# Starting the first expert's first layer before the routing of a mixture-of-experts kernel is complete

## The chip, the core and the metric

The kernel runs on one core of one Trainium2 chip. The time is the device time of one execution in microseconds (us). The kernel before takes 449.11 us, the median of three runs (448.33 to 449.34).

## What is computed

Two stages follow each other. The first is a gated recurrent attention over 4 batches x 8 heads x 768 steps x 48 numbers; its output, regrouped, is a matrix `x` of 3072 rows (tokens) by 384. The second sends every row to one of eight experts, each a two-layer network of 384 to 1024 to 384:

```python
def _moe_ref(x, w_gate, w1, w2):
    logits = x @ w_gate
    expert_idx = np.argmax(logits, axis=1)
    probs = softmax(logits)                     # [shortened]
    gate_w = probs[np.arange(N), expert_idx]
    for e in range(E):                          # [shortened: the rows of e]
        h = np.maximum(x_sorted[lo:hi] @ w1[e], 0.0)
        y_sorted[lo:hi] = h @ w2[e]
    return gate_w[:, None] * y
```

With the seeded inputs the eight experts get 420, 387, 356, 354, 404, 409, 352 and 390 rows. Of the 420 rows of the first expert, 274 lie among the first 2048 tokens.

## The kernel before

**Attention.** The 3072 tokens are 24 chunks of 128. A loop over `s` runs the parts of several chunks side by side, in the order in which the program lists them: `attend(s)`, `scores(s + 1)`, `cums(s + 3)` and so on. Each chunk ends with its rows written to a buffer in device memory, `x_rows` (`x_d`), together with the negated router logits.

**Routing.** Rows are counted per expert in groups of chunks. For each chunk two one-hot matrices, `oh_r` and `oh_c`, say in which slot of which expert a token lands; a product of the two per chunk, summed over all 24 chunks in one PSUM tile (`route`), turns "slot of a token" into "token of a slot". From that the table `g_idx` of row numbers is made, and GpSimd gathers the rows of each block of 128 slots with one indirect DMA.

The slots of the experts follow one another: the first expert has room for 448 rows (three and a half blocks), the next ones for 384, 448 and so on, 26 blocks in all.

```python
caps = (448, 384, 448, 384, 416, 416, 416, 416)
...
s = NT - 1                                  # the last chunk
attend(s)
route = rps.tile([C, Dm], F32, name="cum")
while hots:
    one_hots(hots.pop(0))
tokens_of_slots(0, 9)                       # 9 products into route
slots_of(*rank_products(groups_of[-2], ...))
rows(s)
keep_rows(s)
choose(groups_of[-1])
one_hots(hots.pop(0), nc.gpsimd)
one_hots(hots.pop(0))
tokens_of_slots(9, NT - 3)                  # 12 products
slots_of(*rank_products(groups_of[-1], ps.tile([C, NP, C], F32, name="sB")[:, 0, :E]))
keep_busy(4)                                # 4 products of zeros, not used
one_hots(hots.pop(0))
tokens_of_slots(NT - 3, NT)                 # 3 products
nc.tensor.matmul(route[:, NC : NC + E], lhsT=ones_sq[:], rhs=ohs[:, NT, :], ...)
keep_busy(8)                                # 8 products of zeros, not used
slots(0)                                    # g_idx of the first expert
```

**Experts.** A block gathered is turned (three transposes on TensorE into one PSUM tile of three `128x128` pieces, of which there are two in turn, and a copy by VectorE into `xT`). Then the first layer of an expert, 8 strips of 3 products each; then the second layer block by block, 8 products each, scaled by ScalarE and scattered to the output by GpSimd.

```python
def turn(xg, j, *to):
    tp = mps.tile([C, DB, C], F32, name="xtp")          # two buffers
    for a in range(DB):
        nc.tensor.transpose(tp[:, a, :], xg[:, j, a * C : (a + 1) * C], ident[:])
    for t, at, c0, c1 in to:
        nc.vector.tensor_copy(t[:, :, at : at + c1 - c0], tp[:, :, c0:c1])

def layer1(w1, xT, cols, begun=(), c0=0):
    h = wk.tile([C, FB, CAP], F32, name="h_sb")
    for f in range(FB):
        hp = begun[f] if f < len(begun) else hidden_tile()
        products1(w1, xT, hp, f, c0 if f < len(begun) else 0, cols)   # 3 products
        ...                                                # relu on VectorE or ScalarE

lots = [range(a, b) for a, b in ((0, 7), (7, 13), (13, 20), (20, NBK))]
fetch_lot(0, {begins[i] // C: i for i in (1, 2)})
for i in range(E):
    begun = ()
    if i == 0:
        turn_block(0)
        turn_block(1)
        begun = [hidden_tile() for _ in range(3)]
        for f, hp in enumerate(begun):
            if f == 2:
                turn_block(2)
                turn_block(3)
            products1(w_t[0][0], xT[0], hp, f, 0, 2 * C)
    h_t[i] = layer1(w_t[i][0], xT[i], caps[i], begun, 2 * C)
    if i + 1 < E:
        for k in needed[i + 1]:                            # three blocks, once four
            turn_block(k)
    ...                                                    # weights of later experts
    for n, k in enumerate(ended[i]):
        ...
        results(k)                                         # second layer of block k
        ...
```

Of the kernel before, what the change touches and what calls it, by code (L numbers as in the profile page):

```python
# [8 lines left out]
F32 = mybir.dt.float32  # L9
# [9 lines left out]
def kernel(  # L19
# [9 lines left out]
    out: bass.AP,  # L29
):  # L30


# [53 lines left out]
    groups_of = [range(a, b) for a, b in zip(ends, ends[1:])]  # L86
    ORD = NT - 5


# [120 lines left out]

    xg_pools = [ctx.enter_context(tc.tile_pool(name="moe_x0", bufs=1))]


    wpool = ctx.enter_context(tc.tile_pool(name="wpool", bufs=3))
    w_t = {}

    def fetch1(ex, later=False):
        w1 = wpool.tile([C, DB, F], F32, name="w1")
        if later:

            nc.vector.memset(w1[:, 0, :1], 0.0)
        nc.sync.dma_start(w1[:], moe_w1[bass.ds(ex, 1)].rearrange("e (a p) f -> p (e a) f", p=C))
        return w1

    def fetch_parts(ex):

        w1 = wpool.tile([C, DB, F], F32, name="w1")
        w2 = wpool.tile([C, FB, Dm], F32, name="w2")
        w_t[ex] = w1, w2
        for a in range(DB):  # L230
            for c in range(0, F, 2 * C):
                nc.sync.dma_start(w1[:, a, c : c + 2 * C], moe_w1[ex, a * C : (a + 1) * C, c : c + 2 * C])
                yield
        for f in range(FB):
            nc.sync.dma_start(w2[:, f, :], moe_w2[ex, f * C : (f + 1) * C, :])
            yield

    def fetch2(ex):
        w2 = wpool.tile([C, FB, Dm], F32, name="w2")
        nc.sync.dma_start(w2[:], moe_w2[bass.ds(ex, 1)].rearrange("e (a p) d -> p (e a) d", p=C))  # L240
        return w2

    order = ctx.enter_context(ExitStack())
# [3 lines left out]
    with tc.tile_pool(name="ld", bufs=6) as ld, \  # L247
         tc.tile_pool(name="work", bufs=2) as work, \
         tc.tile_pool(name="ps", bufs=1, space=PSUM) as ps:
        st = {s: {} for s in range(NT)}  # L250
# [179 lines left out]
        def slots_of(g, pos):  # L430
# [16 lines left out]
            if g[0] == ORD:  # L447
                turns(pos3[0:1, 0, :])

        def turns(first):  # L450

# [31 lines left out]
        def slots(i):  # L483

            b, n = begins[i] // UN, caps[i] // UN
            tv = route[:, :NC].rearrange("p (e k q) -> p e k q", e=E, q=NQ)
            e = nc.vector.value_load(order_i[0:1, i - 1 : i], min_val=1, max_val=E - 1) if i else 0
            for q in range(NQ):
                r = slice(q * UN, (q + 1) * UN)
                u = (q - b) % NQ  # L490
                k, m = (b + u) // NQ, len(range(u, n, NQ))
                to, src = g_idx[r, k : k + m], tv[r, bass.ds(e, 1), :m, u]
                if i == 0 and q % 2:
                    nc.scalar.activation(to, src, AF.Copy, bias=float(N // 2))
                else:
                    nc.vector.tensor_scalar_add(to, src, float(N // 2))

        def do(f, i, *a):
            if 0 <= i < NT:
                f(i, *a)  # L500
# [25 lines left out]
        for s in range(-4, NT - 1):  # L526
# [3 lines left out]
            do(scores, s + 1)  # L530
            ranked = [rank_products(g, st[s]["ranks"][:, : len(g) * E]) for g in groups_of if g[-1] == s - 1]
            do(cums, s + 3)
            keep_busy({-3: 3}.get(s, 0))
            do(operands, s + 3)
            if not ranked:
                for _ in range(min(2, len(hots))):
                    one_hots(hots.pop(0))
# [21 lines left out]

        s = NT - 1  # L560
        attend(s)
        route = rps.tile([C, Dm], F32, name="cum")
        while hots:
# [8 lines left out]
        tokens_of_slots(9, NT - 3)  # L572
        slots_of(*rank_products(groups_of[-1], ps.tile([C, NP, C], F32, name="sB")[:, 0, :E]))
        keep_busy(4)
        one_hots(hots.pop(0))
# [3 lines left out]
        )  # L579
        keep_busy(8)  # L580
        slots(0)


    sm = ctx.enter_context(tc.tile_pool(name="moe_sm", bufs=1))
    xg_pools.append(ctx.enter_context(tc.tile_pool(name="moe_x1", bufs=1)))
    wk = ctx.enter_context(tc.tile_pool(name="moe_wk", bufs=2))
    mps = ctx.enter_context(tc.tile_pool(name="moe_ps", bufs=2, space=PSUM))

# [79 lines left out]

    def gather(idx, n=0, due=None):

        xg = xg_pools[n % 2].tile([C, len(idx), W], F32, name="xg")
        for j, i in enumerate(idx):
            if due and j in due:
                slots(due[j])
            nc.gpsimd.indirect_dma_start(  # L675
                out=xg[:, j, :], out_offset=None, in_=x_d[:, :], in_offset=bass.IndirectOffsetOnAxis(ap=i, axis=0),
            )
        return xg

    def gates(xg, n):  # L680
# [20 lines left out]

    def products1(w1, xT, hp, f, c0, c1):
        for a in range(DB):
            nc.tensor.matmul(  # L704
                hp[:, c0:c1], lhsT=w1[:, a, f * C : (f + 1) * C], rhs=xT[:, a, c0:c1],
                start=(a == 0), stop=(a == DB - 1), skip_group_check=True,
            )

    def hidden_tile():
        return mps.tile([C, CAP], F32, name="hp", bufs=3)  # L710

    def layer1(w1, xT, cols, begun=(), c0=0):
        h = wk.tile([C, FB, CAP], F32, name="h_sb")
        for f in range(FB):
            hp = begun[f] if f < len(begun) else hidden_tile()
            products1(w1, xT, hp, f, c0 if f < len(begun) else 0, cols)
            if f % 2 == 0:
                nc.vector.tensor_relu(h[:, f, :cols], hp[:, :cols])  # L718
            else:
                nc.scalar.activation(h[:, f, :cols], hp[:, :cols], AF.Relu)  # L720
        return h

# [21 lines left out]


    lots = [range(a, b) for a, b in ((0, 7), (7, 13), (13, 20), (20, NBK))]
    xe = sm.tile([1, 2 * NX + 1], I32)
    rows, gw, xT, h_t, w1n, nos = {}, {}, {}, {}, {}, {}

    def fetch_lot(n, due=None):  # L750
        g = gather([g_idx[:, k : k + 1] for k in lots[n]], n, due)
        for j, k in enumerate(lots[n]):
            rows[k] = g, j

    def gates_lot(n):
        g = gates(rows[lots[n][0]][0], len(lots[n]))
        for j, k in enumerate(lots[n]):
            gw[k] = g[:, j : j + 1]
# [5 lines left out]
    def turn_block(k):  # L764
        to = []
        for i in range(E):
            a, b = within(i, k)
            if a < b:
                if i not in xT:
                    xT[i] = wk.tile([C, DB, CAP], F32, name="xT", bufs=3)  # L770
                to.append((xT[i], a - begins[i], a - k * C, b - k * C))
        turn(*rows[k], *to)

# [8 lines left out]
    def weights1(i, later=False):  # L782
        nos[i] = nc.sync.value_load(order_i[0:1, i - 1 : i], min_val=1, max_val=E - 1)
        w1n[i] = fetch1(nos[i], later)

    def weights2(i):
        w_t[i] = w1n[i], fetch2(nos[i])


    ended = [range(begins[i] // C, begins[i + 1] // C) for i in range(E)]  # L790
    needed = [range(-(-begins[i] // C), -(-begins[i + 1] // C)) for i in range(E)]


    fetch_lot(0, {begins[i] // C: i for i in (1, 2)})
    for i in range(E):
        begun = ()
        if i == 0:

            turn_block(0)
            turn_block(1)  # L800
            begun = [hidden_tile() for _ in range(3)]
            for f, hp in enumerate(begun):
                if f == 2:
                    turn_block(2)
                    turn_block(3)
                products1(w_t[0][0], xT[0], hp, f, 0, 2 * C)

        h_t[i] = layer1(w_t[i][0], xT[i], caps[i], begun, 2 * C)
        if i + 1 < E:
            for k in needed[i + 1]:  # L810
                turn_block(k)
        if i == 0:
            for n in (1, 2):
                weights1(n, True)
                weights2(n)
            gates_lot(0)
            for n in range(3, E):
                slots(n)
            rows_out(o_idx[:], g_idx[:])
        if i + 3 < E:  # L820
            weights1(i + 3)
        for n, k in enumerate(ended[i]):
            if k not in gw:
                gates_lot([k in lot for lot in lots].index(True))
            results(k)
            if n == 0 and i and i + 2 < E:

                weights2(i + 2)
        if i in (0, 1, 3):
            n = (0, 1, None, 2)[i] + 1  # L830
            fetch_lot(n)
        if i == 0:
# [5 lines left out]
    with tc.If(nx > 0):  # L838
        gx, ox = extra_slots()
        with tc.For_i(0, nx, 1) as i:  # L840
# [6 lines left out]
            w1, w2 = fetch1(ex), fetch2(ex)  # L847
            xg = gather([gi[:]])
            gw = gates(xg, 1)
            xT = wk.tile([C, DB, CAP], F32, name="xT", bufs=3)  # L850
            turn(xg, 0, (xT, 0, 0, C))
            h = layer1(w1, xT, C)
            layer2([(w2, h, 0, C)], gw[:, 0:1], oi[:], False)
# [28 lines left out]
```

## Time and profile before

| | before |
|---|---|
| time, median of 3 | 449.11 us |
| span of the profiled execution | 448.9 us |
| TensorE busy (products) | 431.3 us, 96% |
| VectorE busy | 146.4 us, 33% |
| ScalarE busy | 104.1 us, 23% |
| GpSimd busy | 138.7 us, 31% |
| last product of the routing | at 149.6 us |
| first product of an expert | at 156.66 us |
| first layer of the first expert ends | at 177.2 us |

In the profile PE is TensorE, DVE VectorE, ACT ScalarE, POOL GpSimd and SP the engine that issues most DMAs. "L704" is line 704 of the kernel. A line of the chain of waits reads: start in us, length in us, what it was, and how many. A matmul of 32-bit numbers stands in the records as two, so "x48" is 24 products. In the timeline [...] lengths there overlap; lengths in the chain don't. "PEclk" is the clock that TensorE was granted, 1.00 being full speed. An average over the span says little here, since the kernel has stages with different limits; the stretch from 140 to 180 us is where the change acts first.

### The profile page before, as it was taken

What the parts mean: (1) busy time and instruction counts of PE and PEld (TensorE: products, weight loads), DVE (VectorE), ACT (ScalarE), POOL (GpSimd) and SP (SyncE); (2) the same over time, 40 slices, a digit from 0 to 9 for tenths busy, and PEclk for the clock granted to TensorE, in tenths of its full rate; (3) what the DMA queues carried; (4) which work ended last, traced back from release to release, by engine and by line L of the source; (5) the groups of instructions that cost most, each with busy time, mean ns of one, the idle gap of its engine ahead of it and who ended that gap; (6) DMA issues with size and microseconds to landing.
All of it is one profiled execution on the core that took longest, in us unless ns stands there. A gap on an engine that the chain in (4) does not pass through costs nothing.

```text
span 448.9 us, 7761 instructions
## 1 busy us (share of the span) xinstructions
PE 431.3 (96%) x2963; PEld 286.3 (64%) x2963; DVE 146.4 (33%) x443; ACT 104.1 (23%) x209; POOL 138.7 (31%) x245
## 2 busy tenths in 40 slices
PE   8999999999999799999999999999999999999992
PEld 5888888888888685555555555555555455455451
DVE  3646767676778522622012101201201101201000
ACT  4555554545542001101111111011111011111110
POOL 4667575556563610151151020024020020020010
PEclk9999999999999989999999999999999999999997
DMA  9999999899634320995632710714620040000010
GB/s 174 190 204 200 215 217 213 189 204 212 132 98 128 116 62 0 338 400 183 242 104 65 278 41 12 243 72 122 224 91 19 3 172 19 0 31 19 1 38 23
DMA packets 128433, 59.40 MB, mean 132 GB/s; under 512 B 110462, under 2 KB 123320, under 8 KB 128394
## 3 DMA queue, kind: packets, MB, share of 16 engines
q1 hardware_dynamic: 116258, 48.87, 40.8%
q0 software_dynamic: 3328, 9.94, 6.8%
q10 hardware_dynamic: 8808, 0.08, 1.1%
q8 instruction: 24, 0.39, 0.4%
q14 instruction: 15, 0.12, 0.1%
HBM read 49.30 MB, written 9.96 MB: 132 GB/s over the span
## 4 chain that ended last, share of the span: by engine, by line
PE 73%; issue 11%; DMA 5%; POOL 4%; DVE 3%; ACT 1%; SPq 1%; ACTq 0%; POOLq 0%
PE hp L704 27%; PE zp L730 23%; PE sA L330 3%; PE tp L317 3%; PE cum L286 3%; PE xr L397 3%; DMA x_rows<-xs 2%; PE y L367 2%; PE xtp L698 2%; PE y L360 2%; POOL out_dram L736 2%; PE kvp L367 1%; PE xr L507 1%; PE kvp L376 1%; DMA k_sb<-in_k_dram 1%
## 5 line engine op out<-in xcount | busy, mean ns | idle before, releaser
L704 PE MATMUL hp<-xT,w 128*128 128x416 f32 (+4 forms) x402 | 137.2, 502 | 0.6 <-DVE xT L700 0.6
L730 PE MATMUL zp<-w,h_sb 128*128 128x384 f32 (+2 forms) x560 | 136.7, 488 | 0.0
L704 PEld LDWEIGHTS hp<-xT,w 128*128 128x128 f32 x402 | 76.8, 193 | 58.8 <-issue 43.0
L730 PEld LDWEIGHTS zp<-w,h_sb 128*128 128x128 f32 (+2 forms) x560 | 73.8, 162 | 59.6 <-issue 17.2
L736 POOL DMA_INDIRECT out_dram<-zo,o_idx x26 | 25.8, 993 | 232.7 <-ACT zo L735 165.6
L718 DVE TENSOR_SCALAR h_sb<-hp 128x416 f32<-128x416 f32 (+2 forms) x32 | 18.9, 592 | 183.1 <-PE hp L704 183.1
L720 ACT ACTIVATE h_sb<-hp 128x416 f32<-128x416 f32 (+2 forms) x32 | 16.6, 517 | 125.9 <-PE hp L704 125.9
L735 ACT ACTIVATE zo<-zp,gw 128x384 f32<-128x384 f32 x26 | 15.1, 581 | 127.9 <-PE zp L730 123.4
L675 POOL DMA_INDIRECT xg<-x_rows,g_idx x26 | 25.1, 966 | 9.2 <-issue 7.0
L330 PE MATMUL sB<-qT,kT 48*128 48x128 f32 x192 | 27.7, 285 | 0.0
L330 PE MATMUL sA<-qT,kT 48*128 48x128 f32 x192 | 27.7, 284 | 0.0
L317 PEld LDWEIGHTS tp<-ident,kqb 128*128 128x128 f32 x192 | 22.4, 141 | 7.2 <-issue 4.2
L309 POOL TENSOR_TENSOR kqb<-k_sb,icp 128x384 f32<-128x384 f32 x24 | 24.1, 1005 | 9.0 <-ACT icp L289 7.0
L397 PE MATMUL xr<-back,yT 128*128 128x104 f32 x192 | 25.1, 273 | 0.0
L317 PE MATMUL tp<-ident,kqb 128*128 128x128 f32 x192 | 24.9, 273 | 0.0
L330 PEld LDWEIGHTS sA<-qT,kT 48*128 48x128 f32 x192 | 23.1, 187 | 2.0 <-issue 0.5
L286 PE MATMUL cum<-ln,cmask 128*128 128x384 f32 x48 | 22.4, 549 | 2.0 <-ACT ln L275 2.0
L310 POOL TENSOR_TENSOR kqb<-q_sb,cp 128x384 f32<-128x384 f32 x24 | 24.2, 1007 | 0.0
L397 PEld LDWEIGHTS xr<-back,yT 128*128 128x128 f32 x192 | 23.3, 192 | 0.1
L330 PEld LDWEIGHTS sB<-qT,kT 48*128 48x128 f32 x192 | 23.1, 187 | 0.0
L337 POOL TENSOR_SCALAR_AFFINE_SELECT dB<-dB 128x512 f32<-128x512 f32 x24 | 15.4, 641 | 22.3 <-ACT dB L336 22.3
L320 DVE COPY qT<-tp 128x512 f32<-128x512 f32 x24 | 16.5, 687 | 15.7 <-PE tp L317 15.3
(156 smaller groups left out, 455.0 us busy)
## 6 DMA issues: line engine op xcount, KB each, us to landing
w<-in_moe_w_dram SPq DMA_DIRECT2D x14, 1536.0 KB
x_rows<-xs SPq DMA_DIRECT2D x24, 196.0 KB
a_sb<-in_alpha_dram SPq DMA_DIRECT2D x24, 192.0 KB
k_sb<-in_k_dram SPq DMA_DIRECT2D x24, 192.0 KB
q_sb<-in_q_dram SPq DMA_DIRECT2D x24, 192.0 KB
vb<-in_v_dram SPq DMA_DIRECT2D x24, 192.0 KB
w<-in_moe_w_dram SPq DMA_DIRECT2D x12, 128.0 KB
w<-in_moe_w_dram SPq DMA_DIRECT2D x8, 192.0 KB
```

Source lines behind the costliest of these rows:

```text
L286: nc.tensor.matmul(cum[:], lhsT=cmask[:], rhs=d["ln"][:], start=True, stop=True)
L309: nc.gpsimd.tensor_tensor(kq[:, 0, :, :D], d["k"][:], heads(d["icp"]), op=ALU.mult)
L310: nc.gpsimd.tensor_tensor(kq[:, 1, :, :D], d["q"][:], heads(d["cp"]), op=ALU.mult)
L317: nc.tensor.transpose(tp[:, p, :], pair(kqb[s % 4][:, i], p), ident[:])
L330: nc.tensor.matmul(t[:, p, :], lhsT=d["kT"][r : r + D, p, :], rhs=d["qT"][r : r + D, p, :], start=True, stop=True,)
L397: nc.tensor.matmul(xr[:, p, :], lhsT=d["yT"][:, p, :], rhs=back[:, p, :], start=True, stop=True)
L675: nc.gpsimd.indirect_dma_start(out=xg[:, j, :], out_offset=None, in_=x_d[:, :], in_offset=bass.IndirectOffsetOnAxis(ap=i, axis=0),)
L704: nc.tensor.matmul(hp[:, c0:c1], lhsT=w1[:, a, f * C : (f + 1) * C], rhs=xT[:, a, c0:c1], start=(a == 0), stop=(a == DB - 1), skip_group_c ...
L718: nc.vector.tensor_relu(h[:, f, :cols], hp[:, :cols])
L720: nc.scalar.activation(h[:, f, :cols], hp[:, :cols], AF.Relu)
L730: nc.tensor.matmul(zp[i * wd : (i + 1) * wd, :], lhsT=h[:, f, c : c + wd], rhs=w2[:, f, :], start=(f == 0), stop=(f == FB - 1), skip_group ...
L736: ins = nc.gpsimd.indirect_dma_start(out=out[:, :], out_offset=bass.IndirectOffsetOnAxis(ap=idx, axis=0), in_=zo[:], in_offset=None, bound ...
```

## The change

The first two blocks of the first expert are to be filled from the first 16 chunks alone, so that they can be gathered and turned, and their first layer be run, while the last chunks are still being routed. If fewer than 256 of the first expert's rows lie in those chunks, the rest of the 256 slots stays empty (`close_early` moves the count up). Early slots and gather are put into steps 17, 20 and 21 of the attention loop; the products take the place of the two `keep_busy` calls of the routing's end. For this the PSUM tiles of the attention are given up earlier and those of the experts opened earlier.

Apart from this, at most two blocks are turned one after the other; further blocks are turned after the first block of the second layer. The blocks are gathered in five lots instead of four, and some buffers are split into two pools, so that part of them can exist during the attention.

```diff
+    TE = ORD - ORD % 4                    # 16 chunks
+    EB = 2
+    EC = EB * C                           # 256 rows
...
+        def close_early(pos):
+            cnt = work.tile([1, 1], F32, name="cnt")
+            nc.vector.tensor_scalar(cnt[:], pos, scalar1=float(EC), scalar2=-1.0, op0=ALU.min, op1=ALU.mult)
+            nc.vector.scalar_tensor_tensor(
+                ohs[0:1, TE, 0:1], in0=cnt[:], scalar=float(EC), in1=ohs[0:1, TE, 0:1], op0=ALU.add, op1=ALU.add,
+            )
+        def early_slots(tv):
+            for t in range(TE):
+                nc.tensor.matmul(
+                    tv, lhsT=oh_r[:, t, :], rhs=oh_c[:, t, : EB * NQ], start=(t == 0), stop=(t == TE - 1), ...
+                )
+            for q in range(NQ):
+                ...                        # four VectorE additions into g_idx
...                                        # slots(0): all four additions on VectorE
+            if s == TE + 1:
+                ...                        # one product: count of the first expert's rows
+                close_early(cnt0[0:1, :])
+            if s == TE + 4:
+                early_slots(st[s]["ranks"][:, : EB * NQ])
             do(cums, s + 3)
...
+            if s == TE + 5:
+                fetch_lot(0)
...
         attend(s)
+        for k in range(EB):
+            tp = ps.tile([C, NP, C], F32, name="tp", bufs=2)
+            for a in range(DB):
+                nc.tensor.transpose(tp[:, a, :], rows_t[k][0][:, k, a * C : (a + 1) * C], ident[:])
+            nc.scalar.copy(xT[0][:, :, k * C : (k + 1) * C], tp[:, :DB, :])
...
-        slots_of(*rank_products(groups_of[-1], ps.tile(...)))
-        keep_busy(4)
+        banks.close()
+        mps = ctx.enter_context(tc.tile_pool(name="moe_ps", bufs=2, space=PSUM))
+        ...                                # first_layer(): the 24 products of 256 columns,
+        ...                                # one for each step of go_ahead; relu on ScalarE
+        go_ahead(1)
+        slots_of(*rank_products(groups_of[-1], mps.tile([C, Dm], F32, name="zp")[:, :E]))
+        go_ahead(4)
...
-        keep_busy(8)
         slots(0)
+        fetch_lot(1, {begins[i] // C - EB: i for i in (1, 2)})
...
-    lots = ... ((0, 7), (7, 13), (13, 20), (20, NBK))
+    lots = ... ((0, EB), (EB, 8), (8, 14), (14, 20), (20, NBK))
...
         if i == 0:
-            turn_block(0) ... products1(...)     # [the start with three strips]
-        h_t[i] = layer1(w_t[i][0], xT[i], caps[i], begun, 2 * C)
-        if i + 1 < E:
-            for k in needed[i + 1]:
+            go_ahead(16)
+            for k in range(EB, needed[0][-1] + 1):
                 turn_block(k)
+            go_ahead(99)
+            layer1(w_t[0][0], xT[0], h_t[0], EC, caps[0])      # the other 192 columns
+        else:
+            ...
+            layer1(w_t[i][0], xT[i], h_t[i], 0, caps[i])
+        coming = list(needed[i + 1]) if i + 1 < E else []
+        for k in coming[:2]:
+            turn_block(k)
...
             results(k)
-            if n == 0 and i and i + 2 < E:
-                weights2(i + 2)
+            if n == 0:
+                for j in coming[2:]:
+                    turn_block(j)
+                if i and i + 2 < E:
+                    weights2(i + 2)
```

## Prediction

> **What bounds the kernel now.** I read the busy shares first, then the chain of waits, then the windows with the granted clock, then timelines of the seam between attention and experts.
>
> ```profile
> PE 431.3 (96%) x2963; PEld 286.3 (64%) x2963; DVE 146.4 (33%) x443; ACT 104.1 (23%) x209; POOL 138.7 (31%) x245
> ```
>
> The chain of waits from 149 to 195 us (start, length, what, how many):
>
> ```profile
> 149.62 0.17 PE cum L478 x3
> ...
> 150.87 1.22 POOL xg L675
> ...
> 152.40 3.03 DMA xg<-x_rows,g_idx
> 155.47 0.56 PE xtp L698 x3
> 156.05 0.57 DVE xT L700
> 156.66 4.37 PE hp L704 x12
> 161.03 0.66 PE xtp L698 x6
> 161.69 15.50 PE hp L704 x54
> 177.19 0.34 PE xtp L698 x3
> 177.55 0.57 DVE xT L700
> 178.16 0.55 PE xtp L698 x3
> 178.71 15.48 PE zp L730 x48
> ```
>
> TensorE is the bound; what can be gained is time in which it does nothing useful or runs slowly. The chain shows two such places. From the routing's last product at 149.62 to the first expert product at 156.66 it leaves TensorE: indices on VectorE and ScalarE, a gather on GpSimd, its DMA, a transpose, a copy. That is 7.0 us without expert work (the busy share hides part of it, since eight unused products fill 3.7 us). And at 177.19 three transposes are followed by a VectorE copy before the next three: the third block turned waits for one of the two PSUM tiles. The waits say the same for all experts together:
>
> ```profile
> PE xtp L698 <- DVE xT L700: 2.3, 7, 0.3
> ```
>
> Seven waits of 0.3 us: one at each of the seven passages to a next expert. The windows around the seam show a third loss, in the clock:
>
> ```profile
> core 0: us, PE busy (x), PEclk, DMA share, GB/s
> 149.60:153.50 3.90, 3.80 (x21) 1.00 0.16 39
> 153.50:156.70 3.20, 1.10 (x7) 0.94 0.60 155
> 156.70:161.10 4.40, 4.40 (x15) 0.65 0.60 168
> 161.10:177.20 16.10, 16.10 (x62) 1.00 0.01 2
> ```
>
> The first expert products run at 0.65 of the clock: 12 records (6 products of 256 columns) took 4.37 us, where at full clock they take 2.6.
>
> [...] from the last unused product (ends at 153.4) to the first expert product (156.66) only two groups of transposes run, 3.3 us, and the clock falls. [...] The trace says 3.0 to 4.5 us from issue to landing in this stretch (median 3.1), and I use the trace. [...] The new products need a bank whose last reader is done; which one is a point of risk below.
>
> **Product times used.** From the chain, at full clock: 48 records of 384 columns in 15.48 us, of 416 in 16.76, of 448 in 18.04, so 0.839 ns per column and record. A product (two records) of 256 columns is then 0.43 us. For 192 columns I look whether weight loading (190 ns per record) would hold it up: the 15.50 us of the x54 stretch hold 6 records of 256 (1.29), 30 of 448 (11.27) and 18 of 192, for which 2.94 us remain, 0.163 each. It isn't held up.
>
> **Part 1: the seam.** Before, from 149.62 to the end of the first layer at 177.19: 27.6 us. In the changed order TensorE does in that place: 16 products of 256 columns (5 of the 24 lie before, in place of the four unused ones), 16 x 0.43 = 6.9; six transposes, 0.66; 3 products, 1.3; 24 products of 192 columns, 48 x 0.163 = 7.8. Sum 16.6, saving **10.9 us**, if nothing waits. Can blocks 2 and 3 be there in time? Their gathers are now the first two after `slots(0)`, which before started at 150.87 and 152.40; with about 3.1 us each to land, 154.2 and 155.5, and all four additions on VectorE take as long as two and two (about 0.75 us). TensorE wants them 6.9 us after 149.62, at 156.5. About 1 us to spare. No idle window remains, so no clock loss; it is part of the 10.9.
>
> **Part 2: what is paid earlier.** TensorE fills the windows from 124 to 142 us (6.00 of 6.00), so what is put there counts in full. Sixteen early slot products: the like products of the routing stand 0.055 us apart (12 in 0.83, less the 0.22 of one), 16 x 0.055 = 0.9 us. VectorE's four additions then, 4 x 0.19 = 0.75 us, beside it: VectorE has 5.33 of 6 busy in 130 to 136 and gets 0.9 us more room. At step 17, about 114 us, the chain runs over VectorE (one-hot matrices), so the count and its two small operations cost about 0.4. The two gathers, 2.5 us on GpSimd, come after the masking of chunk 22, which before ended at 137.74 and was followed by 2.44 us of idling: hidden. They land about 3 us after issue, some 1.5 us before their transposes. Those six transposes (0.66) follow chunk 23's attention at 144.1; there TensorE idled 0.41 us for VectorE's copies, so they cost 0.25. The fifth product ahead of the last ranks waits for the bank of `xr`, read by ScalarE until 147.22, and may push the ranks by 0.1. Sum **1.65 us**.
>
> **Part 3: two blocks at most in a row.** Before, each passage took 178.71 - 177.19 = 1.52 us for nine transposes. Six in a row take 0.66 (161.03), three more 0.34: 1.00. Saving 0.52 at six passages, and at the one with four blocks (1.99 before at 283.06) 1.99 - 1.32 = 0.67: **3.8 us** in all. The first product of the second layer doesn't need the copies, and the third block's copy has over 10 us before its use.
>
> Sum: 10.9 - 1.65 + 3.8 = 13.05 us; 449.1 - 13.05 = **436.0 us**.
>
> **Rivals.**
> - *A wait takes the place of the one removed.* Block 3's gather also waits for `slots(1)` on VectorE, done at 151.96 before; its second gather started at 152.40, so there is nearly no room. If blocks 2 or 3 land 1 to 2 us late, TensorE waits that long: 437 to 438. If moreover the first expert product has to wait for a bank whose reader is late, another us.
> - *The attention becomes longer than the sum says.* Steps 17 to 23 run with VectorE at up to 89% and TensorE full. If the early products stop the alternation of the two, VectorE stands behind them, and its copies hold up the scores of the next step: 1 to 3 us more, 437 to 439. For it speaks that in the tail from 141.5 on the chain runs through VectorE; against it that the early additions add less than the products give.
> - *Weights come late.* All later work moves forward by 9 to 13 us; if the experts' weights were fixed in time, the gain would end at the second expert and the time would be about 445. Against it: the fetch of the next weights is released after the turns, at 179.4 before, with over 14 us until first use at 194.19, and the transfer runs near 390 GB/s, 4 us for 1.5 MB. It moves with the turns. I give it little.
> - *Overflow.* Empty slots in the early blocks could push the first expert over 448 and start the extra blocks. It has 274 early rows (256 are wanted), so nothing stays empty: no effect.
>
> **Range and chances.** The known terms are read off contiguous TensorE work, so the gain should not exceed 14.5 us; the uncertain ones (Part 2 and the first two rivals) can take 1 to 4 us. Eight times in ten I expect 434.3 to 439.0. A gain of 2% is 9.0 us, 440.1: to miss it, a third of the sum has to be lost. Faster by over 2%: 0.92; within 2%: 0.07; slower: 0.01.
>
> **What would show each step.** In the profile after: first expert products before the last slot products, at about 149; between 150 and 168 the clock at 1.00 and no TensorE idling over 0.3 us (Part 1); the first layer of the first expert ending near 168.0 instead of 177.2; the last slot product at about 151.2 instead of 149.6 (Part 2); the seven waits of `xtp` on `xT` gone and 1.0 us of turning per passage (Part 3). The prediction is wrong if TensorE waits for blocks 2 and 3 or for the early gather, if the attention's end moves by more than 3 us, or if a weight wait shows at the second expert.

## The result, and the profile after

The changed kernel takes 438.41 us (median; 438.01 to 438.60), the kernel before, beside it on the same chip, 449.23. The ratio is 0.9761, with a 95% interval of 0.9744 to 0.9778: 10.8 us less, where 13.05 were expected.

Busy times, from the page of the kernel after:

```profile
PE 422.0 (97%) x2986; PEld 285.6 (65%) x2986; DVE 147.2 (34%) x454; ACT 107.1 (25%) x218; POOL 138.9 (32%) x245
```

TensorE is still the bound, with 9.3 us less to do: the unused products and the slow first products are gone. The chain of waits of the kernel after, over the same seam as the one shown of the kernel before (start, length, what, how many):

```profile
149.04 0.49 ACT xs L434
...
149.57 0.70 PE hp L647 x2
...
150.30 1.83 PE hp L647 x8
152.14 0.17 PE cum L528 x3
...
152.31 7.01 PE hp L647 x32
159.32 0.66 PE xtp L776 x6
159.98 1.30 PE hp L647 x6
161.28 7.80 PE hp L784 x48
169.07 0.65 PE xtp L776 x6
169.73 5.16 PE zp L800 x16
174.89 0.33 PE xtp L776 x3
175.22 10.32 PE zp L800 x32
```

No other engine is in it any more between 149.57 and 185. Expert products (`hp`, two records each) stand on both sides of the last slot products (`cum` x3), and blocks 2 and 3 are turned (`xtp` at 159.32) without a wait. Only the first product has a wait ahead of it, and the waits of TensorE name it:

```profile
PE sA L360 <- DVE lgn L429: 0.4, 1, 0.4
...
PE hp L647 <- ACT xs L434: 0.3, 1, 0.3
```

The first expert product waits 0.3 us for ScalarE, the last reader of the bank that it takes over. (Its 0.70 us, where a product in a full stream takes 0.43, are those of work that follows a wait: in the kernel before, three transposes took 0.56 us after a wait and six 0.66 without one.) The seven waits of `xtp` on `xT` are not in the list. The windows over the seam show the clock in the column after the busy times:

```profile
core 0: us, PE busy (x) PEld busy (x) DVE busy (x) ACT busy (x) POOL busy (x), PEclk, DMA share, GB/s
149.50:152.40 2.90, 2.83 (x17) 2.38 (x18) 1.97 (x12) 0.41 (x2) 1.59 (x3) 1.00 0.21 75
152.40:159.30 6.90, 6.90 (x34) 6.02 (x34) 1.83 (x12) 1.92 (x5) 4.79 (x5) 1.00 0.39 105
159.30:161.30 2.00, 2.00 (x15) 1.81 (x13) 1.26 (x3) 0.38 (x1) 1.00 (x2) 1.00 0.48 147
161.30:169.10 7.80, 7.80 (x50) 7.78 (x50) 1.44 (x5) 1.38 (x4) 0.00 (x0) 1.00 0.09 26
```

TensorE is full and its clock is 1.00 throughout. The first layer of the first expert ends at 169.07 us and the last slot products start at 152.14, each about 1 us later than the prediction named (168.0 and 151.2).

The two profiled executions differ by 448.9 - 436.7 = 12.2 us, and three pieces make it up. The start of the last slot products moved from 149.62 to 152.14: +2.5. From there to the end of the first layer it was 27.57 and is 16.93: -10.6. From there to the end of the span it was 271.7 and is 267.6: -4.1. The profiled execution of the kernel before happens to be one in which the clock fell at the seam (it took 450.81 us); the other executions don't all lose it, as the experiments show first.

### The profile page after: what moved, and what is told of

Read it like the earlier page. It is cut to its first block, busy times and chain, and to the rows that moved or that the text cites. A ratio compares the mean times of both kernels' runs of the same rounds, so it can differ in the third digit from the quotient of the medians.

```text
span 436.7 us, 7832 instructions
## 1 busy us (share of the span) xinstructions
PE 422.0 (97%) x2986; PEld 285.6 (65%) x2986; DVE 147.2 (34%) x454; ACT 107.1 (25%) x218; POOL 138.9 (32%) x245
## 4 chain that ended last, share of the span: by engine, by line
PE 58%; issue 28%; POOL 4%; DMA 3%; DVE 2%; SPq 1%; ACT 1%; POOLq 0%; ACTq 0%; DVEq 0%
PE zp L800 15%; PE hp L784 13%; PE sA L360 4%; PE xr L427 4%; PE tp L347 4%; PE cum L316 4%; POOL out_dram L806 3%; PE y L397 3%; PE hp L647 2%; PE y L390 2%; PE kvp L397 2%; PE kvp L406 2%; PE xtp L776 1%; DMA k_sb<-in_k_dram 1%; POOL xg L258 1%
## 5 line engine op out<-in xcount | busy, mean ns | idle before, releaser
L784 PE MATMUL hp<-xT,w 128*128 128x416 f32 (+3 forms) x384 | 125.1, 486 | 0.0
L784 PEld LDWEIGHTS hp<-xT,w 128*128 128x128 f32 x384 | 71.7, 190 | 52.0 <-issue 37.8
L789 DVE TENSOR_SCALAR h_sb<-hp 128x416 f32<-128x416 f32 (+3 forms) x32 | 17.9, 558 | 149.1 <-PE hp L784 142.2
L791 ACT ACTIVATE h_sb<-hp 128x416 f32<-128x416 f32 (+3 forms) x32 | 15.7, 491 | 106.7 <-PE hp L784 102.7
L778 DVE COPY xT<-xtp 128x384 f32<-128x384 f32 (+3 forms) x29 | 13.1, 485 | 46.5 <-PE xtp L776 46.3
```

Source lines behind the costliest of these rows:

```text
L784: nc.tensor.matmul(hp[:, c0:c1], lhsT=w1[:, a, f * C : (f + 1) * C], rhs=xT[:, a, c0:c1], start=(a == 0), stop=(a == DB - 1),)
L789: nc.vector.tensor_relu(h[:, f, c0:c1], hp[:, c0:c1])
```

## The experiments

Eleven runs follow. Those under one heading shared one chip and the runs of the kernel before.

### First: the parts one by one

Two theories. A: the parts are worth what the prediction says and add up. B: they do, but something outside them costs a microsecond or two. The rivals of the prediction (blocks late, weights late) were already out by the profile after.

**The kernel before once more**, without an edit.

> The kernel before, unchanged, for a second profile of it. The two profiles show a difference of spans of 12.2 us (448.9 to 436.7), the medians of the times one of 10.8 us (449.23 to 438.41); the execution profiled before had taken 450.81 us, 1.6 us over its median. If that execution was merely a long one, this profile has a span of about 447.5 us, and the part that is missing lies ahead of the routing's end (its last product near 148.2 us instead of 149.6), with the seam (27.6 us) and the passages (1.52 us each) unchanged. If profiles of this kernel always add something, the span is 448.9 us again. Time ratio 1.000.

Measured: 450.26 us, ratio 1.0002 (0.9981 to 1.0024), the same within the interval. Neither of the expected spans came (447.5 or 448.9 us): it is 450.8, the last slot products start at 151.28, and the seam takes 27.8. But the executions fall into two groups. Ten of its 20 have a mean granted clock of 0.992 or more, median 448.87 us, and ten one below that, median 451.5. Counted over all unchanged runs of the kernel before in the three groups of runs, 40 of 87 lie below 0.992; within each of these they are the longer ones, by 1.1 to 2.6 us in the median. Where a profile exists, the mean clock and the seam go together: three profiles with a mean of 0.990 or 0.991 (the kernel before twice, and moved by 32 bytes further below) have 4.37, 4.54 and 4.54 us for the first 12 expert records, two with 0.992 or more (two turns only, clock kept) 2.86.

**At most two blocks in a row, alone.**

```diff
-        if i + 1 < E:
-            for k in needed[i + 1]:
-                turn_block(k)
+        coming = list(needed[i + 1]) if i + 1 < E else []
+        for k in coming[:2]:
+            turn_block(k)
...
+            if n == 0:
+                for j in coming[2:]:
+                    turn_block(j)
```

> The kernel before with the second part of the change alone: at most two blocks turned in a row, the rest after the first block of the second layer. By the sum of the prediction 3.8 us less, 445.4 us; the seven waits of xtp on xT (2.3 us) gone and a passage at 1.00 us of turning instead of 1.52. If turning in the middle of the second layer costs the product stream something of its own (rival), the gain is only the 2.3 us of the waits or less, 446.9 us.

Measured: 445.56 us, ratio 0.9893 (0.9856 to 0.9931). In its profile the time from the end of the first layer to the end of the span is 267.65 us, as in the kernel after, against 271.71 before: 4.08 us for the seven passages. The chain of waits of this kernel shows them, and something not asked for:

```profile
155.25 0.56 PE xtp L698 x3
155.81 0.02 issue
155.83 0.57 DVE xT L700
...
156.44 2.86 PE hp L704 x12
159.30 0.65 PE xtp L698 x6
159.95 15.50 PE hp L704 x54
175.45 0.65 PE xtp L698 x6
176.11 5.16 PE zp L730 x16
181.27 0.33 PE xtp L698 x3
```

The passage is 0.65 + 0.33 us with no copy in it. And the first 12 records took 2.86 us here, not 4.37: the seam has the same wait as before, but in this execution the clock did not fall (1.00 in the window of these 12 records).

**The changed kernel with all turns in a row**, that is, the seam alone.

```diff
-        for k in coming[:2]:
+        for k in coming:
             turn_block(k)
...
-                for j in coming[2:]:
-                    turn_block(j)
```

> The changed kernel with all blocks of the next expert turned in a row as before; the early first layer stays. By the sum 3.8 us more than the changed kernel, 442.2 us, that is 7.0 us less than before. If the two parts help each other (the third block's copy on VectorE collides with the gates and slots of the first expert), the loss is over 5 us; if the early first layer alone brings all, it is under 2 us.

Measured: 443.12 us, ratio 0.9857 (0.9829 to 0.9885). From the end of the first layer to the end it takes 271.73 us again, and the seven waits are back in its list of TensorE's waits:

```profile
PE xtp L776 <- DVE xT L778: 2.3, 7, 0.3
```

Against the kernel before's 449.81 beside them the two parts alone bring 4.25 and 6.69, together 10.9. That is the whole of the changed kernel's gain: within the intervals, of 1.3 to 1.7 us to either side, the parts add. But the seam with its early work was to bring 10.9 - 1.65 = 9.25 and brings 6.7.

**The kernel before with its clock kept**: unused products of 256 columns beside the first turns, so that the 3.3 us without products are broken up: the longest stretch left is 0.9 us, from 157.00 to 157.94.

```diff
-        keep_busy(8)
+        keep_busy(10)
...
             turn_block(0)
+            for _ in range(2):
+                nc.tensor.matmul(warm[:, : 2 * C], lhsT=still[:, :C], rhs=still[:], ...)
             turn_block(1)
+            ...                            # and one more
```

> The kernel before with five more unused products of zeros where TensorE waits for the first two gathered blocks: two more after the routing, two between the turns of block 0 and block 1 and one after them, 2.2 us of work in 3.3 us of waiting. It separates the two losses of the seam: the clock stays up, the waiting stays. Theory: the first expert products run at full clock, 2.6 instead of 4.37 us for six of them, so 1.7 us less, 447.5 us, and of the 10.9 us that the seam gives, the filled wait is 9.2 and the clock 1.7. Rival: the clock falls for another reason (the gathers, transposes), then 449.2 us and 0.65 of the clock as before; or the unused products delay the turns, then up to 1 us more.

Measured: 449.36 us, ratio 0.9994 (0.9974 to 1.0013). In all 20 executions the mean clock was 0.992 or more; in its profile the first 12 expert records take 2.86 us, and they start 0.4 us later for the added products. The expected 447.5 us was missed, since it took the loss for certain; a gain of 0.7 in the mean less these 0.4 is too small for the times to show. So the clock loss is worth 4.37 - 2.86 = 1.5 us where it occurs (1.7 in two other profiles), it occurs in just under half of the executions, and its mean is 0.7. The prediction had booked the full loss for every execution.

That explains 0.8 us of the missing 2.6 or so, not all.

### Second: what is paid earlier

Measured from VectorE's masking in step 17 of the attention loop (`dA`, of chunk 18 counted from 0) to the last slot products, the unchanged and partly changed kernels before take 35.9 to 36.4 us (four profiles), those with the early slots 37.7 to 38.2 (the changed kernel twice, and the one with all turns in a row): in the mean 1.8 us more, where 1.65 was expected. The next runs split this.

**The changed kernel again**, without an edit.

> The changed kernel, unchanged, for more times and a second profile. Two theories of why the medians show 10.8 us and not the 13.05 of the sum. Theory A: the clock loss of the seam, counted in full (1.6 us), happens in some executions only (19 of 44 of the kernel before had a mean granted clock under 0.992), so on the average the change takes away 0.7 us of it, not 1.6; no execution of the changed kernel falls under 0.992. Theory B: the attention itself has become longer ahead of step 17. By A the masking of step 17 (dA) starts within the range of the kernel before (113.3 to 116.0 us in four profiles), and the ratio stays at 0.976; by B it starts about 1 us later in each profile of the changed kernel than in the middle of that range (114.4).

Measured: 438.77 us, ratio 0.9787 (0.9760 to 0.9813): a gain again, but here the interval takes in less than 2%. One of the six executions (441.60 us) has a mean clock of 0.989, against theory A; of 39 executions of kernels with the early first layer two lie below 0.992, and where in the span these lost their clock was not profiled. The masking of step 17 starts at 113.99 us, as theory A has it. Yet over four profiles of the kernel before and its variants this event lies anywhere in 2.7 us (113.3 to 116.0), too wide to rule out a loss of 1 us ahead of it; the third group of runs finds one.

**Without the count** of the first expert's early rows. It leaves out the move that would be needed with fewer than 256 early rows; with these inputs (274) the move is by zero.

```diff
-            if s == TE + 1:
-                cnt0 = st[s]["ranks"][:, :1]
-                nc.tensor.matmul(cnt0, lhsT=ones_sq[:], rhs=ohs[:, TE, 0:1], ...)
-                close_early(cnt0[0:1, :])
```

> The changed kernel without the count at step 17 (one product, two small VectorE operations and the correction of the row count); with this input, where 274 rows stand for 256 slots, the correction is zero. The prediction gave it 0.4 us; the trace of the changed kernel shows VectorE's chain of step 17 longer by about 0.7 (the second operation takes 0.55 us, and the one-hot matrices after it 1.0 us each). If it stands on the path: from the masking of step 17 to the last slot product 37.5 us instead of 38.1, and 0.4 to 0.7 us less in all. If TensorE and the loads hide it, nothing.

Measured: 437.83 us, ratio 0.9754 (0.9728 to 0.9780), 0.9 us less than the changed kernel beside it, with overlapping intervals; in the profile 37.1 us from step 17 on, 0.6 to 1.1 less than in the three with the count. The prediction had put 0.4. From `dA` of step 17 to that of step 18 it takes 5.66 us with the count and 5.15 without. The timeline of the kernel after shows what stands there, with GpSimd's masking beside it:

```profile
114.67 0.64 POOL L367 TENSOR_SCALAR_AFFINE_SELECT dB<-dB 128x512 f32<-128x512 f32 x1 [2.47 <-ACT dB L366]
114.77 0.55 DVE L484 SCALAR_TENSOR_TENSOR ohs<-cnt,ohs 1x1 f16<-1x1 f32 x1
```

An operation on a single element takes 0.55 us, and the one-hots of the chunk stand behind it. The one before it, which makes `cnt` and is as small, is listed with 0.14, and the same kind of operation on seven elements (`key`, in the kernel before at 138.12 us, while GpSimd idles) with 0.15. In all seven profiles with the count the long one ends within 0.02 us of the GpSimd instruction beside it: here of `dB`, and in the two trimmed kernels below, where it stands elsewhere and takes 0.30 and 0.32, of `kqb`. So its length looks like a wait for GpSimd; no run took that neighbour away. The rest of the difference comes in the steps after and differs between profiles of the same program: it isn't traced to an instruction.

**Five times the early slot products**: the same 16 products done five times over, the sum started anew each time, so that the result is the same and 64 products more are run.

```diff
-            for t in range(TE):
+            for t in range(5 * TE):
+                t = t % TE
```

> The changed kernel with the sixteen early slot products done five times over (64 more). The prediction took 0.055 us each from the like products of the routing, 3.5 us more here; the trace of the changed kernel shows the sixteen in 0.49 us, 0.031 each, which gives 2.0 us more. If VectorE's four additions after them, delayed, hold up the scores of the next steps, another 0.5 us or more. So 440.4 us by the trace, 441.9 us by the prediction's figure.

Measured: 440.15 us, ratio 0.9804 (0.9781 to 0.9827), 1.4 us more than the changed kernel. In the chains of waits 16 of them take 0.49 us in the kernel after and 80 take 2.09 here: 0.025 us each. The prediction had taken 0.055 from products with more columns: those have 128, these 8. So the 16 products cost 0.4 and not 0.9.

**Trimmed**: the count's second operation after the reduction of the chunk's rows, the last ranks' bank opened first, and the gather of block 0 one step earlier.

```diff
+            if s == TE + 4:
+                fetch_early(0)
             if s == TE + 5:
-                fetch_lot(0)
+                fetch_early(1)
+            if s == TE + 1:
+                move_up(early_cnt)         # second half of close_early
...
+        last_ranks = mps.tile([C, Dm], F32, name="zp")[:, :E]
-        go_ahead(1)
-        slots_of(*rank_products(groups_of[-1], mps.tile(...)[:, :E]))
+        go_ahead(2)
+        slots_of(*rank_products(groups_of[-1], last_ranks))
```

> A version meant to beat both kernels: the changed kernel with (a) the second VectorE operation of the count after the row reduction of its step instead of ahead of the one-hot matrices, (b) the bank of the last ranks opened ahead of that of the first expert product, and two expert products ahead of the ranks instead of one, (c) the gather of block 0 one step earlier, so that the gather of block 1 is issued 1.25 us earlier. Theory: (a) 0.5 us, (b) 0.4 us; (c) only takes away a wait that some executions may have (0.3 us in one profile). Together 0.9 us less, 437.5 us. Rival: the gather ahead of the rows' copy delays GpSimd's masking and so the scores, 0.5 us more, and the sum is about nothing.

Measured: 438.14 us, ratio 0.9769 (0.9751 to 0.9787). From step 17 on it takes 37.0 us, 0.7 to 1.2 less than the kernels with the untrimmed count, though one more expert product (0.43 us) is done in there; step 17 takes 5.17 us again, so the 0.5 us that the count cost in it are gone. The wait of the first expert product on ScalarE is still there (0.3), so opening another bank first did not avoid it. In the median 0.6 us are gained where 0.9 were expected, within the width of the intervals. Which of the three trims brings how much was not tried.

With all this the early work is accounted for, and there were still 1 to 2 us that no part explained.

### Third: the loads of q, k and alpha

Part of the rest lies where the diff changes no operation: in the first 20 us. The same stage in two profiles, from the windows; the columns at the end are clock, share of the 16 DMA engines (the packets' times added up, so it can exceed 1), GB/s. Before:

```profile
0.00:20.00 20.00, 17.99 (x146) 13.84 (x148) 9.15 (x36) 9.96 (x19) 10.69 (x20) 1.00 0.95 180
```

After:

```profile
0.00:20.00 20.00, 16.45 (x130) 12.77 (x134) 9.04 (x36) 9.36 (x18) 9.87 (x19) 1.00 1.18 178
```

Nearly the same bytes take a quarter more of the DMA engines' time. (TensorE's busy time in this window, 17.99 and 16.45 us, does not tell the versions apart: other profiles of both lie near 17.5.) The hardware queue's line on the page says it of the whole span (packets, MB, share of 16 engines). Before:

```profile
q1 hardware_dynamic: 116258, 48.87, 40.8%
```

After:

```profile
q1 hardware_dynamic: 116258, 48.87, 44.3%
```

Not a packet more, but 0.408 x 448.9 = 183 us of all engines before and 0.443 x 436.7 = 193 after. What differs for these packets is where they land. (In the traces the 98304 packets of 192 bytes hold the whole difference: 95.3 us of all engines before and 106.5 after, the others 125 in both.) The split of buffers into two pools in the changed kernel moves the tiles of q, k and alpha during the attention: their first byte within a partition is 156800 before, a multiple of 64, and 153504 after, an odd multiple of 32. The rows written are 192 bytes long. Three runs put the placement to the test. The spare tile moves the attention's working tiles along with those of q, k and alpha.

**The changed kernel with the tiles put back**: an unused tile in front of them.

```diff
+    SPARE = 824
...
-    with tc.tile_pool(name="ld", bufs=6) as ld, \
+    with tc.tile_pool(name="spare", bufs=1) as spare, \
+         tc.tile_pool(name="ld", bufs=6) as ld, \
...
+        nc.vector.memset(spare.tile([C, SPARE], F32, name="spare")[:, :1], 0.0)
```

> The changed kernel with an unused tile of 824 floats per partition ahead of the tiles of q, k and alpha during the attention, which puts those tiles back at the byte where the kernel before has them (156800 within a partition, a multiple of 64, and not 153504, which is an odd multiple of 32). Theory A, placement: [...] this is the 0.8 us by which all six profiles of changed-type kernels start the fourth cumulative product later. Then the fourth product starts again at 16.4 to 16.7 us (17.2 to 17.4 in those), the hardware queue's packets take about 40.8% of the span's engine time again as in the kernel before and not 44%, and the time falls by 0.8 to 1.5 us to about 437.2. Theory B, not the placement but the changed order of early instructions: fourth product at 17.3, packets at 44%, 438.4 within 0.4.

Measured: 436.67 us, ratio 0.9732 (0.9711 to 0.9753), against 438.77 for the changed kernel on the same chip in the second group of runs. (The two groups can be compared: with the clock kept, the kernel before took 448.07 us in the second and 447.92 in this one.) The two lines, for this kernel; window:

```profile
0.00:20.00 20.00, 18.24 (x140) 13.74 (x140) 9.20 (x37) 9.76 (x19) 10.29 (x19) 1.00 0.96 186
```

and page:

```profile
q1 hardware_dynamic: 116258, 48.87, 41.9%
```

0.419 x 434.9 = 182 us: back at the value of the kernel before. The fourth cumulative product starts at 16.80 us (16.70 in the next kernel), not at 17.22 to 17.43 as in the six changed kernels without the spare tile.

**The trimmed kernel with the same spare tile.**

> The trimmed version (count after the row reduction, last ranks' bank opened first, first gather one step earlier) with the same unused tile. Trimmed alone: 438.14. Theory A: the placement's 0.8 to 1.5 us come off on top, about 436.9, below both kernels; fourth product at 16.4 to 16.7 us. Theory B: 438.1 unchanged. What the trims themselves bring is put at 0.3 to 1.0 us (last chunk's passage 37.0 against 38.0 in the profile, 0.3 us in the median).

Measured: 435.73 us, ratio 0.9719 (0.9697 to 0.9740). It is 2.4 us less than the trimmed kernel without the spare tile, and the fastest of all versions.

**The kernel before with its tiles moved by 32 bytes**: `SPARE = 8`, else the same edit.

> The kernel before, with nothing changed but an unused tile of 8 floats (32 bytes) per partition ahead of the tiles of q, k and alpha, which then start at byte 156832, an odd multiple of 32 as in the changed kernel. Theory A, placement: what the changed kernel suffers appears here by itself: fourth cumulative product at 17.2 to 17.4 us and not 16.4 to 16.7, the hardware queue's packets at about 43 to 44% of the span's engine time and not 40.8%, and 0.8 to 1.5 us more than the kernel before, 450.2 to 450.8 beside 449.3. Theory B: the same as the kernel before within 0.5 us in all three.

Measured: 451.75 us, ratio 1.0050 (1.0024 to 1.0075). Here too the two lines of this kernel; window:

```profile
0.00:20.00 20.00, 17.04 (x126) 13.00 (x130) 9.05 (x37) 9.36 (x18) 9.81 (x19) 1.00 1.18 178
```

and page:

```profile
q1 hardware_dynamic: 116258, 48.87, 42.4%
```

The share of 1.18 of the changed kernel is there without the change, and 0.424 x 450.9 = 191 us on the queue (the share of 42.4% is below the 43 to 44 expected). The fourth cumulative product starts at 17.26 us, as expected. The median exaggerates, because five of its seven executions have a mean clock below 0.992 and five of twelve of the kernel before beside it: like with like, it is 449.1 against 447.9 with the clock kept (two executions only) and 451.8 against 449.3 with it lost.

One event sums it up, the start of VectorE's masking of the second chunk, in all 13 profiles:

| tiles start at | kernels | `dA` of the second chunk |
|---|---|---|
| byte 156800 | before, twice; two turns only; clock kept | 17.36 to 17.65 us |
| byte 156800 | changed or trimmed, with the spare tile | 17.65 and 17.75 us |
| byte 153504 | changed, six versions | 18.16 to 18.38 us |
| byte 156832 | before, moved by 32 bytes | 18.20 us |

The placement decides, not the program. It costs 1.2 to 2.5 us of the time by the four comparisons (the changed kernel, the trimmed one, and the kernel before with its clock kept and with it lost), against the 0.8 to 1.5 expected. In the profiles it is seen up to the thirteenth chunk, whose masking starts at 78.6 to 79.2 us in the six profiles with byte 156800 and at 79.6 to 80.2 in the seven others, 1.0 apart in the mean. At the next two chunks single profiles of both kinds lose up to 3.5 us more, so where the rest of the 1.2 to 2.5 goes is not shown.

What in the placement makes the packets slower is not shown. In the traces 98 to 99% of the 192-byte packets take 13 to 15 ns in the six profiles with tiles from byte 156800; in the seven others 14 to 22% take longer than that and the rest do not. Only these three first bytes were run, and no longer row.

## Why the prediction was right or wrong

**The bound and the seam (Part 1): right.** The prediction's sum for TensorE's work between the last slot products and the end of the first layer was 6.9 + 0.66 + 1.3 + 7.8 = 16.6; the chain has 7.01, 0.66, 1.30 and 7.80. With the 0.17 of the slot products themselves, which the sum forgot, it is 16.9. Blocks 2 and 3 came in time, so the first rival, a new wait, was left at 0.3 us for a bank.

**The clock, inside Part 1: an event booked as a certainty.** "No idle window remains, so no clock loss; it is part of the 10.9" took one profiled execution for all. In 40 of 87 executions of the kernel before the mean clock shows the fall; in the profile of the kernel with two turns only it stayed at 1.00 after the same idle stretch (3.27 us from the last unused product to the first expert product, 3.26 in the kernel before). What decides whether it falls is not shown. The term was 1.5 us where it occurs and 0.7 in the mean: the seam brings 10.6 with the loss and 26.06 - 16.93 = 9.1 without, about 9.8 in the mean and not 10.9.

**What is paid earlier (Part 2): the sum right, two terms wrong in opposite directions.** 1.8 us against 1.65. The 16 early products cost 0.4 and not 0.9 (products of 8 columns were given the price of wider ones); the count costs 0.6 to 1.1 and not 0.4 (0.5 of it from the two VectorE operations in front of the one-hots, the second of which lasts as long as GpSimd's masking beside it). The bank's 0.1 is a wait of 0.3. That the sum still fits is luck. The rival "attention longer by 1 to 3 us" did not come true by the way it names, the early products holding up VectorE: five times as many of them cost 1.4 us, about their own time of 1.6.

**Two turned in a row (Part 3): right.** 4.1 us against 3.8, shown by the part alone and by its removal; the seven waits went and came back.

**Weights and overflow: right to give them little.** No wait for weights is among TensorE's waits in the profile of the changed kernel.

**What the prediction did not have at all** is the placement of the tiles. It read the new pools as a matter of PSUM banks and lifetimes and did not ask where the buffers that stay would land. It takes away 1.2 to 2.5 us of the gain, about 1.0 of it visibly in the first thirteen chunks, whose operations the diff does not touch.

Together: -9.8 at the seam, -4.1 at the passages, +1.8 earlier and +1.2 to +2.5 by placement make -9.6 to -10.9; measured -10.8 and, in the repeat, -10.4. The time is 2.4 us above the 436.0 predicted, inside the range, and with the tiles put back (436.67) it is 0.7 above.

## What to carry to other kernels

Compare the load stages of before and after even where the diff does not touch them: when a change adds or moves pools, print the start of every tile that a DMA fills. Here rows of 192 bytes in tiles from byte 153504 or 156832 cost 1.2 to 2.5 us against byte 156800. Before a wait's side effects, such as a lost clock, enter a prediction, see in several executions whether they always occur. And take the price of a small operation from one of the same size: products of 8 columns took 0.025 us where those of 128 took 0.055. For VectorE look also at what GpSimd does at that moment: one element took 0.55 us in one place and 0.30 in another.

## What the runs showed of the hardware that was not expected

- Moving load targets within a partition, from byte 156800 to 156832 or 153504, raised the DMA engines' share in the first 20 us: it is 0.92 to 0.99 in the six profiles with byte 156800 and 1.07 to 1.18 in the seven others, at about the same GB/s (176 to 188 and 178).
- After an idle stretch of 3.3 us with only transposes in it the clock was 0.62 to 0.65 over the next 4.4 to 4.6 us in three profiles (0.50 from 157.0 to 159.5 us in the kernel before) and 1.00 in another. By the mean clock it fell in 40 of 87 executions; with the unused products in the stretch, in none of 20.
- A one-element VectorE operation ended within 0.02 us of the GpSimd instruction beside it in all seven profiles that have it, and took 0.30 to 0.55 us accordingly.
- An early gather of 128 rows landed 3.0 to 3.9 us after its issue in seven profiles, but in one (the changed kernel with all turns in a row) block 1's took 5.2, and TensorE's weight load waited 0.3 us for it: the sign of error that the prediction named, in one profile and small. The trimmed version issues the gathers at 136.02 and 139.71 us, where the changed kernel has 139.61 and 141.12, and so widens the margin for both blocks.
